# More filler matmuls in the head, and the last tile's large residual add on Pool

## The chip, the cores and the metric

The kernel runs on one core of one Trainium2 chip. A core has five engines with a queue each: PE (TensorE, matmuls), DVE (VectorE), ACT (ScalarE), POOL (GpSimd) and SP, which here only issues DMAs. They run side by side and wait for each other through semaphores. The metric is the device time of one execution in microseconds; the time given is the median over repeated runs. The profile is of one execution.

## The reference

With x of shape [2048, 1024], 32 heads of 32 and bf16 data, the kernel computes

```
xn  = layernorm(x)
q, k, v = split(xn @ wqkv)                       # 32 heads x 32
logits[s, w] = q[s] . k[s - 2w] / sqrt(32)       # w = 0..7, masked where s - 2w < 0
s   = (softmax(logits) over v[s - 2w]) @ wo      # 1024 x 1024
h   = silu(xn @ w1) * (xn @ w3)                  # 1024 -> 3584
g   = silu(h @ w2)                               # 3584 -> 1024
out = x + s * g
```

## The kernel before

The 2048 rows are done in four chunks of 512 (`CH`), each of four tiles of 128 rows (`st`). For a chunk, PE makes q, k and v from the transposed normalized rows `xnT`, then the gate and up products in 14 blocks (`up_block`), then the down product in two halves of 512 output columns (`down_half`), with the attention's output projection (`wo_piece`) in the middle. The attention arithmetic, the layer norm of the next chunk and the closing `x + s * g` are put between PE's groups from a list with costs and due times (`Side`); the program order on each engine is the order in which the code issues the instructions (`manual_schedule`). Weights are streamed by SP through nine buffers. Nothing of this middle part is touched.

*The head* (lines 525 to 583) is written out by hand. There is nothing for PE to compute until the first rows of x are loaded and normalized, so `busy(src, n)` (line 492) issues n filler matmuls, 128 x 512, whose result lands in the PSUM tile `warm_ps` and is never read. Fourteen of them stand at the start. Then comes tile 0: its statistics and normalization on VectorE (`half_stats`, `aggr`, `norm0`, the normalization itself is line 193), eight transposes on PE (`pe_transpose`, line 517), and copies of the transposes from PSUM into `xnT` (`copy_in`, line 521). Six fillers follow the transposes of tile 0. Tile 1 goes the same way, and then the first matmuls of q start on these two tiles (`part`, line 563), with the transposes of tiles 3 and 2 between them. The PSUM pool of `warm_ps`, the transposes and `ps_wo` has two buffers.

*The tail* is `last_half`: for the last chunk, the second half of the down product is made one row tile after another (line 477). For each, ScalarE applies silu out of PSUM (`silu_acc`, line 428), and `finish` does three things: VectorE multiplies with the attention output (line 434), VectorE adds the rows of x (line 435) into a buffer `o_t`, and a DMA on the given queue writes it out (line 436). For the last row tile the output projection is done at the very end, in a piece of 384 columns and one of 128, each followed by its own `finish`; VectorE reads the projection straight from PSUM. Both pieces are written out by the SP queue, the 384-column piece first.

Of the kernel before, what the change touches and what calls it, by code (L numbers as in the profile page):

```python
# [45 lines left out]
def kernel(  # L46
# [11 lines left out]
    nc = tc.nc  # L58
# [4 lines left out]
    CH = 512  # L63
    NCH = S // CH
    NST = CH // P
# [73 lines left out]
    def take_w(item):  # L139
        got, wt = w_tiles.popleft()  # L140
        assert got == item, (got, item)
        return wt
# [6 lines left out]
    x0 = [xp.tile([P, D], BF16, tag="x", name=f"x0_{st}") for st in range(NST)]  # L149
# [39 lines left out]
    def half_stats(x_t, stats, i):  # L189
        nc.vector.bn_stats(out=stats[:, i, :], in_=x_t[:, i * 512:(i + 1) * 512])  # L190
# [214 lines left out]
    def wo_piece(oT, was, st, c0, w):  # L405
        dh, n0 = divmod(c0, CH)
        ps = psum_aux.tile([P, CH], FP32, tag="aux", name="ps_wo")
        for j in range(NJ):
            nc.tensor.matmul(  # L409
                ps[:, 0:w], lhsT=oT[:, j, st * P:(st + 1) * P], rhs=was[dh][:, j, n0:n0 + w],  # L410
                start=(j == 0), stop=(j == NJ - 1),
            )
        return ps
# [12 lines left out]
    def silu_acc(acc, w=512):  # L426
        gt = ep.tile([P, 512], FP32, tag="gt", bufs=5)
        nc.scalar.activation(out=gt[:, 0:w], in_=acc, func=ACTF.Silu)  # L428
        return gt

    def finish(c, st, c0, w, gt, s, xres, queue):
        g0 = (c * NST + st) * P
        o_t = ep.tile([P, 512], BF16, tag="o_t")
        nc.vector.tensor_mul(gt, gt, s)  # L434
        nc.vector.tensor_add(o_t[:, 0:w], gt, xres[:, st, c0:c0 + w])  # L435
        queue.dma_start(out=out_flat[g0:g0 + P, c0:c0 + w], in_=o_t[:, 0:w])  # L436

    def finish_half(c, dh, gts, s_sb, xres, queue):
        def one(st):
            finish(c, st, dh * 512, 512, gts[st][:], s_sb[:, st, dh * 512:(dh + 1) * 512], xres, queue)  # L440
        for st in range(NST):
            side.add(1.38, lambda st=st: one(st))
# [29 lines left out]
    def last_half(c, hts, s_sb, xres, was):  # L472
        w2ts = [take_w(("2", 1, fb)) for fb in range(7)]
        for st in range(NST):
            acc = psum_mm.tile([P, 512], FP32, tag="mm", name=f"acc{c}_1_{st}")
            for f in range(FT):
                nc.tensor.matmul(  # L477
                    acc[:], lhsT=hts[f][:, st * P:(st + 1) * P], rhs=w2ts[f // 4][:, f % 4, :],
                    start=(f == 0), stop=(f == FT - 1),
                )  # L480
            gt = silu_acc(acc[:])
            if st < NST - 1:
                finish(c, st, 512, 512, gt[:], s_sb[:, st, 512:1024], xres, nc.sync)
        for n0, w in ((0, 384), (384, 128)):
            ps = wo_piece(att["oT"], was, NST - 1, CH + n0, w)
            finish(c, NST - 1, CH + n0, w, gt[:, n0:n0 + w], ps[:, 0:w], xres, nc.sync)


    xnT = xnT_pool.tile([P, KT, CH], BF16, tag="xnT")
# [2 lines left out]
    def busy(src, n):  # L492
        for _ in range(n):
            nc.tensor.matmul(wps[:], lhsT=warm[:, 0:P], rhs=src[:, 0:CH], start=True, stop=True)
# [15 lines left out]
    def norm0(st):  # L510
        nc.vector.reciprocal(out=rs0[st][:], in_=rs0[st][:])
        normalize(x0[st], mv0[st][:, 0:1], rs0[st][:])

    def pe_transpose(st):
        tp = psum_aux.tile([P, KT, P], BF16, tag="aux", name=f"tp{st}")
        for kt in range(KT):
            nc.tensor.transpose(tp[:, kt, :], x0[st][:, kt * P:(kt + 1) * P], ident[:])
        return tp

    def copy_in(tp, st, ks, eng):  # L520
        eng(out=xnT[:, ks, st * P:(st + 1) * P], in_=tp[:, ks, :])
# [10 lines left out]
    half_stats(x0[1], st0[1], 0)  # L532
    norm0(0)
    tp0 = pe_transpose(0)
    busy(x0[0], 6)
    copy_in(tp0, 0, HI, A)
    half_stats(x0[1], st0[1], 1)
    aggr(1)
# [2 lines left out]
    half_stats(x0[3], st0[3], 0)  # L541
    norm0(1)
    tp1 = pe_transpose(1)
    half_stats(x0[3], st0[3], 1)
    copy_in(tp1, 1, LO, V)
    copy_in(tp1, 1, HI, A)
# [38 lines left out]
    for j in range(NOPEN, NJ):  # L585
        ps = psum_mm.tile([P, CH], FP32, tag="mm", name="ps_qkv")
# [5 lines left out]
    for c in range(NCH):  # L592
# [15 lines left out]
        xres = res["x"]  # L608
        every = [(dh, st) for dh in range(2) for st in range(NST)]
        if c + 1 < NCH:  # L610
            state = {}

            def mid(fb):
                if fb == WO_AT - 1:
                    state["s"] = wo_proj(every, was)
                    finish_half(c, 0, gts, state["s"], xres, nc.gpsimd)

            gts1 = down_half(c, 1, hts, mid)
            side.flush()
            finish_half(c, 1, gts1, state["s"], xres, nc.gpsimd)  # L620
            xnT = att["x"]
        else:
            s_sb = wo_proj(every[:-1], was)
            finish_half(c, 0, gts, s_sb, xres, nc.gpsimd)
            side.flush()
            last_half(c, hts, s_sb, xres, was)
# [30 lines left out]
```

## Time and profile before

| what | us |
|---|---|
| median of three runs | 819.64 (818.79 to 819.96) |
| the profiled execution | 818.27 |
| its span, first to last instruction | 816.5 |
| PE busy in the span | 809.6 (99%) |
| VectorE busy | 464.8 (57%) |
| ScalarE busy | 191.5 (23%) |
| Pool busy | 92.4 (11%) |
| first real matmul of q starts | 9.72 |
| last product on VectorE of the last tile starts | 813.13 |

In the lines of the profile that follow, a timeline row has the start in us, the duration in us, the engine, the line of the kernel, the operation, output and inputs by the program's names, the shape, and in brackets the idle time of the engine just before it with what ended it. `x6` means six instructions in one row; the duration is then that of the row. PE is the matmuls, PEld the weight loads that go with them, SPq the issuing of DMAs by SP. In a row of grouped instructions the numbers behind the bar are busy us, mean ns of one, and idle time before. Durations of matmuls include the way through the array: what counts for the next matmul is the distance of the starts.

### The profile page before, as it was taken

To read this page: it belongs to the slowest core of one execution; us is meant where nothing else is said; L and a number is where in the kernel's file an instruction comes from. 1 tells how busy PE (TensorE), PEld (TensorE's weight loads), DVE (VectorE), ACT (ScalarE), POOL (GpSimd) and SP (SyncE) were. 2 spreads that over 40 slices of the span, in tenths; PEclk is the share of its full clock that TensorE was granted. 3 is DMA by queue.
4 is the path that set the end of the run, shared out by engine and by line. 5 is a ranking of instruction groups with operands and counts; after the bars stand their busy time and mean duration, and the time that the engine had idled before them with its cause. 6 is when DMAs were issued, how large, how long until landed. Compare 5 with 4: busy or idle time off the path is not lost.

```text
span 816.5 us, 9525 instructions
## 1 busy us (share of the span) xinstructions
PE 809.6 (99%) x3820; PEld 406.2 (50%) x3820; DVE 464.8 (57%) x472; ACT 191.5 (23%) x310; POOL 92.4 (11%) x172
## 2 busy tenths in 40 slices
PE   8999999999999999999999999999999999999997
PEld 6654444444565444444466444444446644444443
DVE  4099574942229765692224968479311694759432
ACT  4331331012332132101133213310223321311120
POOL 0000312001100223000110031400001004130010
PEclk9999999999999999999999999999999999999999
DMA  8476999742366799965245789996424378687500
GB/s 283 136 197 202 212 182 298 242 155 78 104 192 170 221 197 214 296 207 154 78 132 152 190 221 197 210 291 206 142 90 155 104 206 204 165 220 240 177 33 20
DMA packets 190925, 146.39 MB, mean 179 GB/s; under 512 B 19360, under 2 KB 171680, under 8 KB 190880
## 3 DMA queue, kind: packets, MB, share of 16 engines
q1 hardware_dynamic: 185440, 133.71, 59.1%
q0 software_dynamic: 5440, 12.07, 6.4%
q8 instruction: 30, 0.49, 0.3%
q14 instruction: 15, 0.12, 0.1%
HBM read 130.02 MB, written 4.19 MB: 164 GB/s over the span
## 4 chain that ended last, share of the span: by engine, by line
PE 91%; DVE 4%; DMA 2%; issue 1%; ACT 1%; POOL 0%; SPq 0%; DVEq 0%; ACTq 0%
PE gu L245 40%; PE acc L454 20%; PE ps_qkv L245 19%; PE ps_wo L409 7%; PE acc L477 3%; DMA Pr<-pb 2%; PE ps_qkv L563 1%; DVE pv L383 1%; DVE ht L251 1%; DVE stats L190 1%; POOL Pr L372 0%; DMA x<-in_A_x_dram 0%; ACT L249 0%; DVE oT L394 0%; DVE pv L394 0%
## 5 line engine op out<-in xcount | busy, mean ns | idle before, releaser
L245 PE MATMUL gu<-xnT_next,w 128*128 128x512 bf16 x1344 | 290.6, 379 | 0.0
L245 PEld LDWEIGHTS <-w 128*128 128x128 bf16 x1792 | 175.3, 98 | 211.2
L454 PE MATMUL acc<-w,ht 128*128 128x512 bf16 x784 | 170.5, 379 | 0.1
L245 PEld LDWEIGHTS <-wq 128*128 128x128 bf16 x720 | 103.3, 143 | 52.1
L249 ACT ACTIVATE sg<-gu 128x512 bf16<-128x512 f32 x112 | 65.9, 597 | 261.8 <-PE gu L245 242.7
L251 DVE TENSOR_TENSOR ht<-sg,gu 128x512 bf16<-128x512 bf16 x112 | 75.8, 681 | 88.5 <-PE gu L245 70.0
L299 DVE TENSOR_TENSOR prod<-qT,kT 128x4096 bf16<-128x4096 bf16 x32 | 73.1, 2285 | 92.6 <-ACT kT L272 92.6
L245 PE MATMUL ps_qkv<-xnT_next,wq 128*128 128x512 bf16 x576 | 124.8, 379 | 0.0
L454 PEld LDWEIGHTS <-ht 128*128 128x128 bf16 x784 | 76.6, 98 | 92.9 <-issue 0.4
L245 PE MATMUL gu<-xnT,w 128*128 128x512 bf16 x448 | 96.9, 379 | 0.0
L434 DVE TENSOR_TENSOR gt<-gt,s_sb 128x512 f32<-128x512 f32 x31 | 21.4, 690 | 125.2 <-ACT gt L428 67.7
L330 POOL DMA_DIRECT2D L<-E x64 | 37.2, 588 | 273.5 <-DVE E L314 265.6
L383 DVE TENSOR_TENSOR pv<-Pr,vT 128x4096 bf16<-128x4096 bf16 x28 | 63.3, 2283 | 0.0
L310 DVE TENSOR_TENSOR prod<-prod 128x2048 bf16<-128x2048 bf16 x64 | 61.2, 956 | 1.4
L409 PE MATMUL ps_wo<-wo,oT 128*128 128x512 bf16 (+2 forms) x264 | 56.1, 373 | 0.0
L428 ACT ACTIVATE gt<-acc 128x512 f32<-128x512 f32 x32 | 19.1, 597 | 148.8 <-PE acc L454 127.0
L436 POOL DMA_DIRECT2D out_dram<-o_t x28 | 15.4, 549 | 310.5 <-DVE o_t L435 310.5
L372 POOL DMA_DIRECT2D Pr<-pb x64 | 36.8, 582 | 108.7 <-DVE pb L364 99.9
L409 PEld LDWEIGHTS <-oT 128*128 128x128 bf16 x264 | 25.6, 98 | 30.0
L394 DVE TENSOR_TENSOR oT<-oT,pv 128x4096 bf16<-128x4096 bf16 x16 | 36.6, 2287 | 0.2
L421 ACT CAST s_sb<-ps_wo 128x512 bf16<-128x512 f32 x31 | 18.2, 586 | 66.4 <-PE ps_wo L409 66.4
L245 PE MATMUL ps_qkv<-xnT,wq 128*128 128x512 bf16 x144 | 31.2, 379 | 0.0
(64 smaller groups left out, 312.2 us busy)
## 6 DMA issues: line engine op xcount, KB each, us to landing
w<-in_B_w_dram SPq DMA_DIRECT2D x168, 512.0 KB, 5.2
wq<-in_A_wqkv_dram SPq DMA_DIRECT2D x44, 512.0 KB, 3.8
wo<-in_A_wo_dram SPq DMA_DIRECT2D x8, 1024.0 KB, 10.0
L<-E POOLq DMA_DIRECT2D x64, 64.0 KB, 6.1
Pr<-pb POOLq DMA_DIRECT2D x64, 64.0 KB, 5.1
xres<-in_A_x_dram SPq DMA_DIRECT2D x4, 1024.0 KB, 6.2
out_dram<-o_t POOLq DMA_DIRECT2D x28, 128.0 KB, 2.0
x_t<-in_A_x_dram SPq DMA_DIRECT2D x12, 256.0 KB, 6.6
```

The source lines that it names most:

```text
L245: nc.tensor.matmul(ps, lhsT=lhs(kt), rhs=rhs(kt), start=(kt == 0), stop=(kt == KT - 1))
L249: nc.scalar.activation(out=sg[:], in_=g_ps[:], func=ACTF.Silu)
L251: nc.vector.tensor_mul(ht[:], sg[:], u_ps[:])
L299: nc.vector.tensor_mul(prod, qT[:], kT[:, :, o:o + CH])
L310: nc.vector.tensor_add(prod[:, 0:n, :], prod[:, 0:n, :], prod[:, n:2 * n, :])
L330: nc.gpsimd.dma_start(out=L4[sq * NH:(sq + 1) * NH, r, :, :], in_=E_r[r, :, :, sq * P:(sq + 1) * P],)
L372: nc.gpsimd.dma_start(out=Pr_r[r, :, :, sq * P:(sq + 1) * P], in_=pb[sq * NH:(sq + 1) * NH, :, :],)
L383: nc.vector.tensor_mul(dst, Pr[:, w, :].unsqueeze(1).to_broadcast([P, NJ, CH]), vT[:, :, o:o + CH])
L394: nc.vector.tensor_add(a, a, b)
L409: nc.tensor.matmul(ps[:, 0:w], lhsT=oT[:, j, st * P:(st + 1) * P], rhs=was[dh][:, j, n0:n0 + w], start=(j == 0), stop=(j == NJ - 1),)
L454: nc.tensor.matmul(accs[st][:], lhsT=hts[f][:, st * P:(st + 1) * P], rhs=w2t[:, i, :], start=(f == 0), stop=(f == FT - 1),)
L477: nc.tensor.matmul(acc[:], lhsT=hts[f][:, st * P:(st + 1) * P], rhs=w2ts[f // 4][:, f % 4, :], start=(f == 0), stop=(f == FT - 1),)
```

## The change

Two places are edited. In the head, the fillers behind the transposes of tile 0 become ten instead of six, and two fillers are put behind the transposes of tile 1, reading tile 1. In the tail, `finish` gets an argument for the engine of the residual add; for the last row tile, the add of the 384-column piece is done by Pool and that of the 128-column piece still by VectorE. Both products stay on VectorE, both DMAs on the SP queue in the same order.

```diff
-    def finish(c, st, c0, w, gt, s, xres, queue):
+    def finish(c, st, c0, w, gt, s, xres, queue, adder=None):
         g0 = (c * NST + st) * P
         o_t = ep.tile([P, 512], BF16, tag="o_t")
         nc.vector.tensor_mul(gt, gt, s)
-        nc.vector.tensor_add(o_t[:, 0:w], gt, xres[:, st, c0:c0 + w])
+        (adder or nc.vector).tensor_add(o_t[:, 0:w], gt, xres[:, st, c0:c0 + w])
         queue.dma_start(out=out_flat[g0:g0 + P, c0:c0 + w], in_=o_t[:, 0:w])
...
-        for n0, w in ((0, 384), (384, 128)):
+        for n0, w, adder in ((0, 384, nc.gpsimd), (384, 128, nc.vector)):
             ps = wo_piece(att["oT"], was, NST - 1, CH + n0, w)
-            finish(c, NST - 1, CH + n0, w, gt[:, n0:n0 + w], ps[:, 0:w], xres, nc.sync)
+            finish(c, NST - 1, CH + n0, w, gt[:, n0:n0 + w], ps[:, 0:w], xres, nc.sync, adder)
...
     tp0 = pe_transpose(0)
-    busy(x0[0], 6)
+    busy(x0[0], 10)
     copy_in(tp0, 0, HI, A)
...
     tp1 = pe_transpose(1)
+    busy(x0[1], 2)
     half_stats(x0[3], st0[3], 1)
```

## The prediction

> **What bounds the kernel now.** I read the page's busy table first, then the granted clock, then the two ends of the run, since the change touches nothing between them: the timeline and the chain of the first 10 us, and the timeline of the last 5 us.
>
> ```profile
> PE 809.6 (99%) x3820; PEld 406.2 (50%) x3820; DVE 464.8 (57%) x472; ACT 191.5 (23%) x310; POOL 92.4 (11%) x172
> PEclk9999999999999999999999999999999999999999
> ```
>
> PE is busy 99% of the span at the full clock, so from about 10 us to 812 us the time is PE's queue. Only what delays PE's first real matmul, or what lies behind its last one, moves the end. First the head, TensorE's matmuls and then its weight loads:
>
> ```profile
> 5.73 0.62 PE L517 MATMUL tp<-ident,x 128*128 128x128 bf16 x8
> 6.19 1.46 PE L494 MATMUL warm_ps<-x,warm 128*128 128x512 bf16 x6
> 8.59 0.62 PE L517 MATMUL tp<-ident,x 128*128 128x128 bf16 x8 [0.94 <-DVE x L193]
> ...
> 2.91 0.15 PEld L494 LDWEIGHTS <-warm 128*128 128x128 bf16 x1 [0.28 <-issue]
> 3.34 0.15 PEld L494 LDWEIGHTS <-warm 128*128 128x128 bf16 x1 [0.28 <-issue]
> 3.76 1.48 PEld L494 LDWEIGHTS <-warm 128*128 128x128 bf16 x7 [0.28 <-issue]
> ```
>
> The six fillers stand between the first and second transposes, then PE idles 0.94 us until VectorE has normalized the second tile. The weight loads of the start-up fillers come 0.43 us apart up to 3.76 us and 0.21 us apart after it (seven in 1.48 us): the array runs at half rate for its first 2.5 us. The chain through the same stretch:
>
> ```profile
> 7.78 0.17 DVE rs L511
> 7.96 0.03 issue
> 7.98 0.56 DVE x L193
> 8.54 0.05 issue
> 8.59 0.64 PE tp L517 x8
> 9.22 0.02 issue
> 9.24 0.44 DVE xnT L521
> 9.68 0.04 issue
> 9.72 2.78 PE ps_qkv L563 x24
> ```
>
> PE is on it only with the transposes; from 9.72 us on it is PE's own. The 24 matmuls of 256 columns take 2.78 us, that is 0.11 us each, half of the 0.21 us of 512 columns: full rate, in spite of the idle 0.94 us and of the 0.52 us ahead of them. Last the tail, in the timeline:
>
> ```profile
> 812.06 0.55 DVE L434 TENSOR_TENSOR gt<-gt,ps_wo 128x384 f32<-128x384 f32 x1 [5.37 <-PE ps_wo L409]
> 812.65 0.56 DVE L435 TENSOR_TENSOR o_t<-gt,xres 128x384 bf16<-128x384 f32 x1
> 813.13 0.28 DVE L434 TENSOR_TENSOR gt<-gt,ps_wo 128x128 f32<-128x128 f32 x1
> 813.24 0.86 SPq L436 DMA_DIRECT2D out_dram<-o_t  x2
> 813.44 0.29 DVE L435 TENSOR_TENSOR o_t<-gt,xres 128x128 bf16<-128x128 f32 x1
> ```
>
> Four VectorE operations run in a row. SP issues the 384-column piece at 813.24 us and the 128-column piece when VectorE is through (813.73 us): the two issues end at 814.10, each takes 0.33 us by the rows of the output tensor, so the second starts at 813.77. From there to the end of the span (816.5) are 2.73 us: 1.5 us of landing by the issue table, the rest the closing of the program. I take these 2.73 us as fixed.
>
> **The change part by part.** *Four more fillers after the first transposes.* They are 128x512 matmuls at full rate there: starts 0.216 us apart (six start between 6.19 and 7.27 and each is 0.38 long in the rows, which makes the 1.46). The tenth starts at 6.19 + 9 x 0.216 = 8.13 and has left the array at 8.35. The second transposes wait for VectorE until 8.54 and start at 8.59. Cost 0, covered by the idle 0.94 us; 0.24 us of that cover is left. VectorE's normalization and ScalarE's copies of the first transposes wait for no filler, so nothing on the chain before 8.59 moves. If the cover were gone, each filler would cost its 0.216 us.
>
> *Two fillers after the second transposes.* Eight transposes start 0.056 us apart from 8.59, the last has passed at 9.04. The fillers hold the array from 9.04 to 9.47. VectorE's copy of the transposes is released by the last transpose, not by the fillers, so it keeps 9.24; the first real matmul waits for that copy and starts at 9.72. Cost 0, cover 0.25 us. Behind the fillers stand the weight load of the first wq matmul (0.15 us at 8.99 now; it fits between 9.3 and 9.72) and all of PE's queue. The filler bank is now freed only at about 9.63 instead of 7.65; the next user is the third transposes at 12.34, and the next writer of the second x tile is a load at 73.6 us, so neither waits. Twelve instructions more on PE are inside these sums.
>
> *The 384-column add moved from VectorE to Pool.* VectorE loses 0.56 us: its 128-column product starts at about 812.6 instead of 813.13 and its 128-column add ends at about 813.2. Pool has been idle since its last output DMA at 785.25 + 0.54 us, so it starts when VectorE's product is done: 812.61 plus 0.05 for the signal, 812.66. Pool's other waits (x's residual tile, the older users of the output buffer, whose transfer was issued at 800.68) are long satisfied, and nothing is queued behind the add on Pool. But SP's queue keeps its order: the 384-column DMA now waits for Pool, and the 128-column DMA waits behind it although its data are ready. With T for Pool's add, SP issues the first at 812.68 + T and the second 0.37 us later (0.33 for the issue, 0.04 for the wait), at 813.05 + T. Before, it was 813.77. So the end moves by **T - 0.72 us**.
>
> T is not in the trace. Pool's rows, and VectorE's row for the same operation:
>
> ```profile
> L278 POOL COPY kT<-kT 128x128 bf16<-128x128 bf16 x3 | 0.9, 303 | 0.0
> L641 POOL MEMSET const-float32-0.0<- 128x1 f32 x1 | 0.1, 100 | 0.2 <-issue 0.2
> L435 DVE TENSOR_TENSOR o_t<-gt,xres 128x384 bf16<-128x384 f32 x1 | 0.6, 557 | 0.0
> ```
>
> Lower end: VectorE's pace, 0.56 us, a gain of 0.16. Pool's copy gives 0.10 fixed and (303 - 100)/128 = 1.6 ns per column with one input: 0.10 + 384 x 1.6 ns = 0.71 us, no change. Twice the slope for two inputs: 1.32 us, 0.60 us slower. The add reads two inputs, so it is nearest to the last two rows; I take their middle, T = 1.0 us: **+0.28 us**, with -0.16 and +0.60 as ends. Where VectorE's 128-column add meets Pool's on the memory and waits for it, it ends 0.29 us after Pool, still ahead of SP's second issue slot 0.37 us after Pool.
>
> [...]
>
> *Sum.* 0 + 0 + 0.28 us. The profiled execution took 818.27 us (span 816.5 and 1.77 outside it) and becomes 818.55; the median of the three timed runs is 819.64, 1.37 above it. On the median: **819.9 us**. A difference of 0.2% (1.64 us) is about what a measurement of this kernel can tell from no change, and this one is far inside it.
>
> **The rivals.** *Pool is as quick as VectorE* (T = 0.56): 819.64 - 0.16 = 819.5. For it: Pool's memsets and selects take 0.2 to 0.3 us, no more than VectorE's small operations. Against: its copy of 128 bf16 columns takes 303 ns, more than VectorE's add of 128 (292).
>
> *The fillers overrun the gap* (the other side). The place is the second transposes at 8.59. Here the array reached full rate at 3.8 us; in one us at half rate PE loses 0.49 us of work (2.3 fillers done instead of 4.6). PE is ready for the first transposes 0.10 us early (the fourteenth filler leaves at 5.58, VectorE delivers at 5.68), and the ten fillers leave 0.24. So from a full rate that comes 0.34/0.49 = 0.7 us later, at 4.5 us, the added fillers delay the chain, up to all four at half rate, 4 x 0.43 = 1.7 us: 820.2 to 821.6. For it: start-up is part of every execution. Against: the one execution shown has the cover.
>
> [...] This trace has the half rate for 2.5 us; a later release in other runs is not shown by it.
>
> *The idle time costs clock in the timed runs, and the fillers save it.* The timed runs lie 0.5 to 1.7 us above the profiled one. A fall to half rate as long as that of the start (2.5 us) costs 1.27 us; all of it saved gives 819.92 - 1.27 = 818.6, and a longer fall would give 818.0. For it: that spread. Against: the full rate at 9.72 here.
>
> *Pool's first add has a start-up.* The nearest price of a first use is ScalarE's table load, 1.28 us in the rows of this trace: 821.2, and more if Pool's is dearer. Against: Pool's first copies and selects here show 0.3 us and no gap. [...]
>
> **How the numbers follow.** Forecast (T between 0.7 and 1.3, head hidden) 0.52; Pool quick 0.08; overrun 0.15, of which 0.06 is beyond 821.28; clock saved 0.12, of which 0.06 is below 818.0; start-up 0.13, of which 0.12 is beyond 821.28. Slower 0.06 + 0.12 = 0.18, faster 0.06, within 0.2% the other 0.76. The range runs from the clock saved (818.6) to the middle of the slow cases (821.4); what it leaves out is most of the start-up and the tips of the other two.
>
> **What would show it.** In the changed profile: ten fillers from 6.19 and the second transposes still at 8.59 behind VectorE's normalization; two fillers ahead of 9.72 and matmuls from 9.72; in the tail a Pool add of about 1 us from 812.66, and SP's two issues back to back, the second near 814.05. Wrong it is if the transposes wait for fillers, if PE's matmuls after 9.72 run at 0.21 us each, or if Pool's add is several us long or starts late.

## The result, and the profile after

The changed kernel takes 820.87 us (median of 20 runs, 819.71 to 822.75) against 819.68 us before (20 runs, 818.66 to 820.77). The ratio is 1.0016 with a 95% interval of 1.0009 to 1.0022, that is 0.7 to 1.8 us slower: inside 0.2%, but four times the 0.28 us that the sum gave. The profiled execution has a span of 818.5 us against 816.5 and took 820.30 us against 818.27. So 2.0 us have to be found between these two executions.

The head first: TensorE's matmuls of the changed kernel in the timeline, then the chain of the same stretch.

```profile
5.94 0.62 PE L517 MATMUL tp<-ident,x 128*128 128x128 bf16 x8 [0.22 <-DVE x L193]
6.39 2.32 PE L494 MATMUL warm_ps<-x,warm 128*128 128x512 bf16 x10
8.55 0.61 PE L517 MATMUL tp<-ident,x 128*128 128x128 bf16 x8
9.00 0.59 PE L494 MATMUL warm_ps<-x,warm 128*128 128x512 bf16 x2
```

```profile
5.94 0.62 PE tp L517 x8
6.56 2.16 PE warm_ps L494 x10
8.71 0.46 PE tp L517 x8
9.18 0.02 issue
9.20 0.44 DVE xnT L521
```

The fillers fit, but only just: the idle 0.94 us ahead of the second transposes has become nothing, and the chain now runs through the ten fillers. VectorE delivered the first tile at 5.88 us instead of 5.68 in this execution, which moved the fillers 0.2 us later and used up the cover. VectorE delivered the second tile at 8.43 us, 0.10 earlier than before; the fillers then hold its transposes for about 0.07 us, to 8.55. The first real matmul starts at 9.68 us (9.72 before): the head cost less than 0.1 us here.

The tail of the changed kernel in the timeline:

```profile
812.83 0.75 DVE L434 TENSOR_TENSOR gt<-gt,ps_wo 128x384 f32<-128x384 f32 x2 [5.37 <-PE ps_wo L409]
813.47 0.91 POOL L435 TENSOR_TENSOR o_t<-gt,xres 128x384 bf16<-128x384 f32 x1 [27.80 <-DVE gt L434]
813.61 0.91 DVE L435 TENSOR_TENSOR o_t<-gt,xres 128x128 bf16<-128x128 f32 x1
814.40 0.81 SPq L436 DMA_DIRECT2D out_dram<-o_t  x2
```

Pool's add takes 0.91 us. VectorE's add of 128 columns, which waits for nobody in the program, takes 0.91 us too, instead of 0.29. Counted from the start of the 384-column product (812.06 before, 812.83 now), the two output DMAs are all issued 2.38 us later (814.40 + 0.81 - 812.83) instead of 2.04 (813.24 + 0.86 - 812.06): 0.34 us more. From the same point to the end of the span it is 5.7 us instead of 4.4, 1.2 to 1.3 us more. So about 0.9 us are lost behind the last DMA issue, in the stretch that the prediction took as fixed. The closing instructions, by their line, show them. Columns: number, shortest/median/longest in ns, first and last start. Before:

```profile
L652 POOLq EVENT_SEMAPHORE  x4: 17/17/17, 815.8 to 816.4; - x4
L652 POOLq DRAIN  x3: 40/98/3908, 785.2 to 816.2; - x3
L652 SPq DRAIN  x3: 7/7/7, 815.7 to 816.0; - x3
```

And after:

```profile
L653 POOLq EVENT_SEMAPHORE  x4: 17/17/17, 817.8 to 818.4; - x4
L653 POOLq DRAIN  x3: 40/98/4315, 813.4 to 818.3; - x3
L653 SPq DRAIN  x3: 7/7/7, 816.8 to 818.0; - x3
```

Pool's queue ends with a drain, here an instruction that starts beside Pool's last work and ends well behind it, and the engines meet (the rows of semaphores) only after it. In the changed kernel the drain starts at 813.43 and lasts 4.32 us, to 817.74: Pool's add ended at 814.38, so the drain goes on for 3.36 us behind it. SP has the landings and is ready at 816.8; Pool comes at 817.8. Before, the same drain stands at 785.2 and lasts 3.91 us, to 789.1: Pool's last instruction, a DMA issue, ended at 785.79, again 3.35 us earlier. There it lay 26 us ahead of the end and cost nothing. SP comes 0.35 us later against the product, Pool 0.9 us later than SP: together the 1.2 to 1.3 us.

What is left of the 2.0 us is not in either edit. The changed kernel's timeline has one gap on TensorE in the middle of the run:

```profile
552.39 0.68 DVE L251 TENSOR_TENSOR ht<-sg,gu 128x512 bf16<-128x512 bf16 x1
552.98 2.29 DVE L394 TENSOR_TENSOR oT<-oT,pv 128x4096 bf16<-128x4096 bf16 x1
553.12 1.67 PE L454 MATMUL acc<-w,ht 128*128 128x512 bf16 x7 [0.91 <-DVE ht L251]
```

VectorE made that `ht` 0.76 us later than before (552.39 against 551.63), because it had waited 7.7 us instead of 6.9 for the DMA of `Pr` ahead of 537 us. None of the edits touches this stage, so I take it for a difference between two executions; no run was made for it alone. The other traces bear this out: from the first real matmul to the 384-column product it is 802.34 us in the profile of before and 803.15 in that of the change, and between 802.4 and 803.3 us in the other traces, whatever was edited (but for the last kernel of the table below, whose matmuls start at half rate).

### The profile page after: what moved, and what is told of

Its sections match the earlier page's. It is cut to its first block, busy times and chain, and to the rows that moved or that the text cites. A ratio compares the mean times of both kernels' runs of the same rounds, so it can differ in the third digit from the quotient of the medians.

```text
span 818.5 us, 9463 instructions
## 1 busy us (share of the span) xinstructions
PE 806.8 (99%) x3752; PEld 406.8 (50%) x3826; DVE 464.8 (57%) x471; ACT 191.4 (23%) x310; POOL 92.9 (11%) x173
## 4 chain that ended last, share of the span: by engine, by line
PE 90%; DVE 4%; DMA 2%; issue 2%; POOL 0%; ACT 0%; SPq 0%; DVEq 0%; ACTq 0%
PE gu L245 39%; PE acc L454 20%; PE ps_qkv L245 19%; PE ps_wo L409 7%; PE acc L477 3%; DMA Pr<-pb 2%; PE ps_qkv L564 1%; DVE pv L383 1%; DVE ht L251 1%; DVE stats L190 1%; POOL Pr L372 0%; DMA w<-in_B_w_dram 0%; DMA x<-in_A_x_dram 0%; ACT L249 0%; DVE oT L394 0%
```

## The experiments

All were timed against the kernel before on the same chip. "Product to end" is the time from the start of VectorE's 384-column product to the end of the span, in the profiled execution: it leaves out the head and the middle.

| kernel | median us | before us | ratio (95%) | product to end |
|---|---|---|---|---|
| before | | | | 4.4 |
| the change | 820.87 | 819.68 | 1.0016 (1.0009 to 1.0022) | 5.7 |
| fillers alone | 819.56 | 819.24 | 1.0005 (0.9997 to 1.0014) | 4.4 |
| Pool add alone | 820.15 | 819.24 | 1.0013 (1.0004 to 1.0022) | 5.7 |
| idle Pool copy | 820.57 | 819.24 | 1.0016 (1.0007 to 1.0025) | 5.3 |
| Pool add one tile earlier | 818.96 | 819.24 | 0.9997 (0.9988 to 1.0005) | 4.5 |
| sixteen fillers | 820.70 | 819.05 | 1.0021 (1.0013 to 1.0030) | 4.4 |
| Pool adds the 128 columns | 820.78 | 819.05 | 1.0024 (1.0015 to 1.0033) | 6.05 |
| second DMA on ScalarE's queue | 820.53 | 819.05 | 1.0016 (1.0007 to 1.0025) | 5.7 |
| no fillers behind tile 0 | 819.63 | 819.05 | 1.0012 (1.0003 to 1.0021) | 4.4 |
| ten at the start, six | 818.96 | 819.37 | 0.9994 (0.9985 to 1.0004) | 4.4 |
| ten at the start, four | 819.12 | 819.37 | 1.0000 (0.9991 to 1.0009) | 4.4 |
| eight at the start, none | 820.69 | 819.37 | 1.0018 (1.0008 to 1.0029) | 4.4 |

### The two parts, each alone

```diff
-    busy(x0[0], 6)
+    busy(x0[0], 10)
...
     tp1 = pe_transpose(1)
+    busy(x0[1], 2)
```

> The fillers alone (ten behind the first transposes, two behind the second), both adds of the tail on VectorE. Theory (the tail makes the difference, by the drain of Pool at the close): the second transposes start at most 0.1 us after VectorE delivers, the first real matmul at 9.6 to 9.8 us, the median within 0.2 us of before. Rival (the fillers delay PE by a late start of the full rate): 0.8 to 1.2 us slower than before, with the fillers on the chain and the real matmuls starting at 10.5 us or later.

By the times, the fillers alone cost -0.25 to +1.15 us: no difference that can be told, and not enough for the whole. But the profiled execution shows what the rival had described. The chain through its head:

```profile
2.69 4.58 PE warm_ps L494 x11
7.26 0.45 PE tp L517 x8
7.71 2.16 PE warm_ps L494 x10
9.87 0.46 PE tp L517 x8
```

And two of the weight loads, with the first transposes behind them:

```profile
5.89 0.15 PEld L494 LDWEIGHTS <-warm 128*128 128x128 bf16 x1 [0.28 <-issue]
6.32 0.15 PEld L494 LDWEIGHTS <-warm 128*128 128x128 bf16 x1 [0.28 <-issue]
6.75 0.15 PEld L517 LDWEIGHTS <-x 128*128 128x128 bf16 x1 [0.28 <-DVE mv L505]
```

All fourteen start-up fillers ran 0.43 us apart; the first record of the full clock is at 7.0 us instead of 3.9. The first transposes start at 7.10, and the ten fillers hold the second ones until 9.71, although VectorE had delivered at 9.31: 0.4 us lost to the added fillers, in this execution. With six fillers the late clock costs less: in the kernel with the early Pool add, below, the full clock came at 6.8 us, the first transposes stood at 7.00, the second at 9.26, right behind VectorE's 9.21, and the first real matmul at 10.40. So neither expectation had the head right: the real matmuls started at 10.83, as the rival said, but the larger part of that delay is the late clock, which six fillers meet too.

```diff
-        nc.vector.tensor_add(o_t[:, 0:w], gt, xres[:, st, c0:c0 + w])
+        (adder or nc.vector).tensor_add(o_t[:, 0:w], gt, xres[:, st, c0:c0 + w])
...
-        for n0, w in ((0, 384), (384, 128)):
+        for n0, w, adder in ((0, 384, nc.gpsimd), (384, 128, nc.vector)):
```

> The Pool add alone, six fillers as before. Drain theory: Pool's add of 0.91 us, then a drain on Pool's queue of about 3.37 us behind it, and the closing waits for that drain: Pool ends 0.9 + 3.4 = 4.3 us after VectorE's product, against 3.1 us from the product to the closing of before, so 1.2 us slower than before. Rival (the price is the longer add and SP's order alone): second output DMA 0.35 us later and 0.35 us slower in all.

The Pool add alone is 0.3 to 1.8 us slower and has the same 5.7 us from product to end as the whole change. Its tail and its closing lines:

```profile
812.34 0.75 DVE L434 TENSOR_TENSOR gt<-gt,ps_wo 128x384 f32<-128x384 f32 x2 [5.37 <-PE ps_wo L409]
812.98 0.91 POOL L435 TENSOR_TENSOR o_t<-gt,xres 128x384 bf16<-128x384 f32 x1 [27.12 <-DVE gt L434]
```

```profile
L652 POOLq EVENT_SEMAPHORE  x4: 17/17/17, 817.3 to 817.9; - x4
L652 POOLq DRAIN  x3: 40/98/4315, 812.9 to 817.8; - x3
L652 SPq DRAIN  x3: 7/7/7, 816.3 to 817.5; - x3
```

SP is ready at 816.3, Pool at 817.3. The time is in the tail, and the larger part of it is the wait for Pool.

### A Pool instruction that no output waits for

```diff
         for n0, w in ((0, 384), (384, 128)):
             ps = wo_piece(att["oT"], was, NST - 1, CH + n0, w)
             finish(c, NST - 1, CH + n0, w, gt[:, n0:n0 + w], ps[:, 0:w], xres, nc.sync)
+            if n0 == 0:
+                nc.gpsimd.tensor_copy(out=spare[:], in_=gt[:, 0:8])
```

> Before, with a Pool copy of 8 columns of the 384-column product into a spare buffer that nobody reads; it is extra work and no output waits for it. Drain theory: the copy takes 0.1 to 0.2 us from 812.7, the drain lasts to about 816.2 us, Pool then comes 0.4 to 0.5 us after SP, and the run is 0.4 to 0.5 us slower than before although the output DMAs stand where they stood. Rival (only what the output waits for counts): no difference from before.

```profile
813.26 0.55 DVE L435 TENSOR_TENSOR gt<-gt,ps_wo 128x384 f32<-128x384 f32 x1 [5.37 <-PE ps_wo L410]
813.85 0.56 DVE L436 TENSOR_TENSOR o_t<-gt,xres 128x384 bf16<-128x384 f32 x1
813.88 0.58 POOL L489 COPY spare<-gt 128x8 f32<-128x8 f32 x1 [27.12 <-DVE gt L435]
814.43 0.85 SPq L437 DMA_DIRECT2D out_dram<-o_t  x2
```

```profile
L655 POOLq EVENT_SEMAPHORE  x4: 17/17/17, 817.9 to 818.5; - x4
L655 POOLq DRAIN  x3: 40/98/3963, 813.9 to 818.3; - x3
```

The output DMAs stand where they stood (all issued 814.43 + 0.85 - 813.26 = 2.02 us after the product's start, 2.04 before), and yet the end comes 0.9 us later and the run is 0.6 to 2.0 us slower. The drain ends 3.36 us behind the copy, as behind the add. This rules out that the add's length or SP's order is the main price. The sum behind 0.4 to 0.5 us was short because the copy of eight columns took 0.58 us where I had put 0.1 to 0.2: it ends 0.05 us after VectorE's add beside it.

In the trace of the change it was the other way round: VectorE's add of 128 columns, 0.91 instead of 0.29 us, ended beside Pool's add, at 814.52, 0.15 us after Pool's 814.38. In both traces the instruction that started second ended just after the other engine's. What holds it up no trace shows, and no run has that copy with VectorE idle beside it.

### The same add, early enough

```diff
-                finish(c, st, 512, 512, gt[:], s_sb[:, st, 512:1024], xres, nc.sync)
+                finish(c, st, 512, 512, gt[:], s_sb[:, st, 512:1024], xres, nc.sync, nc.gpsimd if st == 2 else None)
```

> Pool adds the residual of the tile before the last (512 columns, at 806 us), VectorE both pieces of the last tile. Drain theory: Pool's add takes about 1.2 us and the drain ends at about 810.7 us, 5 us before the closing: within 0.2 us of before. Rival (a Pool add costs wherever it stands, by a start-up or by holding up VectorE): slower by 0.5 us or more.

```profile
806.81 1.15 POOL L435 TENSOR_TENSOR o_t<-gt,xres 128x512 bf16<-128x512 f32 x1 [20.17 <-DVE gt L434]
```

```profile
L652 POOLq EVENT_SEMAPHORE  x4: 17/17/17, 816.6 to 817.2; - x4
L652 POOLq DRAIN  x3: 40/98/4562, 806.8 to 817.0; - x3
```

Here Pool's add ends at 807.96 and the drain at 806.76 + 4.56 = 811.3, 3.4 us behind it and 5 us before the engines meet (816.6). The time does not differ from before. A Pool add costs nothing that can be told here, where its drain is covered, and no start-up price shows.

### The other piece, and the other queue

```diff
-        for n0, w, adder in ((0, 384, nc.gpsimd), (384, 128, nc.vector)):
+        for n0, w, adder in ((0, 384, nc.vector), (384, 128, nc.gpsimd)):
```

> VectorE adds the 384 columns, Pool the 128 columns of the last piece; six fillers. Drain theory: Pool starts when the 128-column product is done (about 0.8 us later than with the 384 columns), adds for 0.35 to 0.5 us, and its drain of 3.37 us ends about 4.7 us after the 384-column product, so 1.4 to 1.7 us slower than before, although the last DMA is issued only 0.1 to 0.2 us later. Rival (the length of Pool's add and SP's order set the price): 0.1 to 0.3 us slower.

```profile
814.02 1.10 SPq L436 DMA_DIRECT2D out_dram<-o_t  x2
814.33 0.43 POOL L435 TENSOR_TENSOR o_t<-gt,xres 128x128 bf16<-128x128 f32 x1 [28.34 <-DVE gt L434]
```

```profile
L652 POOLq DRAIN  x3: 40/98/3817, 814.3 to 818.6; - x3
```

The add is less than half as long (0.43 us), the last DMA is out 0.2 us later than before by product time, and the run has the largest ratio of the table: 1.2 to 2.7 us slower, 1.6 us in the trace (6.05 against 4.4). Pool ends later, at 814.76, and the drain with it, at 818.1.

```diff
-            finish(c, NST - 1, CH + n0, w, gt[:, n0:n0 + w], ps[:, 0:w], xres, nc.sync, adder)
+            finish(c, NST - 1, CH + n0, w, gt[:, n0:n0 + w], ps[:, 0:w], xres, nc.sync if n0 == 0 else nc.scalar, adder)
```

> The Pool add of the 384 columns, with the 128-column piece written out by the ScalarE queue, so that it does not wait behind the 384-column DMA on SP; six fillers. Drain theory: the outputs are issued 0.4 us earlier than with the Pool add on one queue, and the end does not move against it: still 1.1 to 1.3 us slower than before. Rival (SP's order sets the price): 0.4 us better than with one queue.

```profile
813.27 0.75 DVE L434 TENSOR_TENSOR gt<-gt,ps_wo 128x384 f32<-128x384 f32 x2 [5.37 <-PE ps_wo L409]
814.85 0.33 SPq L436 DMA_DIRECT2D out_dram<-o_t  x1
815.00 0.38 ACTq L436 DMA_DIRECT2D out_dram<-o_t  x1
```

Both outputs are issued by 2.11 us after the product's start instead of 2.38, 0.27 us earlier (0.4 were expected; VectorE's add of 128 columns, again 0.91 us beside Pool's, holds the rest: it ends at 814.96, and ScalarE's queue issues at 815.00). The end does not move: 5.7 us. SP's order is not what sets it.

### The fillers and the clock

```diff
-    busy(x0[0], 6)
+    busy(x0[0], 16)
...
     tp1 = pe_transpose(1)
+    busy(x0[1], 2)
```

> Sixteen fillers behind the first transposes and two behind the second, both adds on VectorE. With a cover of 0.24 us behind ten fillers (before) or none (the changed kernel's trace), six more at 0.216 us delay the second transposes, and with them the first real matmul, by 1.05 to 1.35 us: 1.0 to 1.4 us slower than before. Rival (PE's queue in the head is hidden by something else, such as the loads of wq): less than 0.5 us slower.

```profile
6.35 3.62 PE L494 MATMUL warm_ps<-x,warm 128*128 128x512 bf16 x16
9.80 0.61 PE L517 MATMUL tp<-ident,x 128*128 128x128 bf16 x8
10.93 0.81 PE L564 MATMUL ps_qkv<-xnT,wq 128*128 128x256 bf16 x6
```

The first real matmul moves from 9.72 to 10.93, 1.21 us, and the run is 1.1 to 2.5 us slower. Nothing hides PE's queue in the head once the gap is filled.

```diff
-    busy(x0[0], 6)
```

> Before, without the six fillers behind the first transposes: PE idles about 2.4 us ahead of the second transposes. If idle time there costs clock, the first matmuls of q run at half rate (0.21 us for 256 columns instead of 0.11) and the run is 0.5 to 1.3 us slower. If it does not, no difference from before, and the four added fillers could not have gained anything either.

The profiled execution is untouched: first matmuls at 9.70, 24 of them in 2.81 us. But the runs fall into two groups. Seven of eleven lie between 819.15 and 820.08 us with a mean granted clock of 0.999 or 1.000, four between 821.04 and 821.34 with 0.997 or 0.998. By an estimate from the half rate of these traces, a clock of 0.998 over 818 us is about 3.3 us at half rate, 1.6 us of work. All 33 runs of before beside them lie below 820.5 with 0.999 or more. The profile is of a run of the first group, so no trace shows where in the other four the half rate lies. Nor does 0.998 alone prove it: the mean also counts the closing, where the recorded clock fell to half at 816.25 us in the trace of the change, 3.1 us after the end of the last matmul (0.55 from 816 us to the end), and the kernels with a longer closing have runs at 0.998 that are no slower than their others (four of eleven with two queues). Here the closing is as short as before, 4.4 us.

```diff
-    busy(warm, 14)
+    busy(warm, 8)
...
-    busy(x0[0], 6)
```

> Eight start-up fillers and none behind the first transposes: PE is idle for most of the time from 4.6 to 9.7 us. If busy time in the head is what brings and keeps the full rate, most runs have a mean granted clock of 0.998 or less, the first matmuls of q run at 0.21 us for 256 columns, and the median is 1 to 2 us slower than before. If not, no difference from before.

```profile
5.77 1.04 PE L517 MATMUL tp<-ident,x 128*128 128x128 bf16 x8 [0.94 <-DVE x L193]
8.46 1.04 PE L517 MATMUL tp<-ident,x 128*128 128x128 bf16 x8 [1.65 <-DVE x L193]
10.10 4.12 PE L562 MATMUL ps_qkv<-xnT,wq 128*128 128x256 bf16 x22 [0.61 <-DVE mv L505]
```

The matmuls of q run at half rate, 4.12 us for 22, and the first record of the full clock is at 13.3 us. The run is 0.7 to 2.4 us slower, as expected. The mean clock was expected at 0.998 or less in most runs; six of eight had 0.999 or 1.000. Half rate up to 13.3 us would make the mean about 0.992 over this span of 820 us, and the profiled run has 0.999: the mean counts the time from the first record of the full clock on (3.9 us in the trace of before, whose clock is listed as 1.000), so this late start does not show in it; the pace of the matmuls does.

```diff
-    busy(warm, 14)
+    busy(warm, 10)
```

> Before, with ten start-up fillers instead of fourteen; the six behind the first transposes stay. Reading of the traces so far: in some executions the full rate comes only at 5 to 7 us, the fourteen start-up fillers at 0.43 us each then hold PE up to 7.1 us, and the first transposes start up to 1.4 us late. Ten of them are through by 1.23 + 10 x 0.43 = 5.5 us even at half rate, so the first transposes start at 5.7 to 6.0 us whenever VectorE delivers; 0.2 to 0.6 us faster than before in the median. Rival (fewer fillers lose the full rate, as without the six): a group of runs 2 us slower with a mean granted clock of 0.998, and no gain in the median.

Ten start-up fillers free PE in time: the full clock came at 7.1 us in its profile, and the first transposes started at 5.79, right behind VectorE. But the second ones came at 9.18, because ScalarE had waited until 6.30 us for the third tile's load, and VectorE's second tile hangs on ScalarE's queue: its `rs` waited 0.73 us for ScalarE's, up to 8.38. The median is 0.4 us below before; the interval (-1.2 to +0.3 us) does not tell it from no gain. None of its eleven runs shows 0.998.

```diff
-    busy(warm, 14)
+    busy(warm, 10)
...
-    busy(x0[0], 6)
+    busy(x0[0], 4)
```

> Ten start-up fillers and four behind the first transposes. Reading as for ten and six, and where the full rate comes late four fillers at half rate (1.7 us) end before the second tile is normalized, so 0.2 to 0.6 us faster than before. Rival: the longer idle time ahead of the second transposes costs the full rate in some executions, 2 us each, as seen in 4 of 11 runs without fillers.

No gain that can be told (-0.7 to +0.7 us), and one of eleven runs at 821.22 us with a clock of 0.998. But two of the 25 runs of before beside it, with fourteen and six fillers, show the same: 820.87 and 821.02 us at 0.998. So this does not show that four are too few, and it shows that six do not always keep the clock either.

## Why the prediction was right or wrong

*The range and the sign held*: 820.87 lies in 818.6 to 821.4, within 0.2% of before and above it. That was in part luck. The sum put the change at +0.28 us against 1.19; the range reached up to 821.4 for fillers that overrun and for a start-up of Pool, and what filled it was in the main neither. The missing 0.9 us have, in the main, one cause.

*The term that failed* is the sentence that took the 2.73 us from the last DMA issue to the end of the span as fixed: "1.5 us of landing by the issue table, the rest the closing of the program". The closing is not fixed. It waits for Pool's drain, which ends 3.35 to 3.37 us after Pool's last instruction in twelve of the thirteen traces, be that a DMA issue, an add of 128, 384 or 512 columns or a copy of 8; in the thirteenth (ten at the start, four) it is 3.49 behind a DMA issue. In all thirteen the span ends 0.76 to 0.78 us after the later of two: SP ready with the landings, or Pool's drain. The prediction asked what would be queued behind the add on Pool and answered "nothing"; the drain was queued there. It stood in the profile of before, 3.9 us long at 785.2 us, among the closing instructions, 26 us ahead of the end and so covered by everything. Adding an instruction behind 785 us moved that drain; the idle copy, the early add and the 128-column add show that its place sets the price, not the add. What the drain does in its 3.4 us no trace shows.

*The rest of the tail's sum came out.* T was put at 1.0 us between 0.56 and 1.32; it is 0.91. The second output was predicted 0.28 us later and the issues ended 0.34 us later. That they come so close is partly chance: with the measured T the sum gives 0.19, and Pool's start, the step between SP's two issues and the second issue itself each came out 0.04 to 0.06 us longer than put. Against VectorE's 0.557 us for the same add, Pool's 0.907 us is a factor of 1.63. Three sizes give 0.43, 0.91 and 1.15 us: 1.9 ns per column and 0.19 us fixed.

*VectorE's second add* was allowed to wait for Pool's. It took 0.6 us longer beside it (0.91 against 0.29 us) and ended 0.15 us after it, not 0.29; that the two meet on the memory no trace shows. It was right that this stays hidden behind SP's order: the add ends at 814.52, and SP's second issue starts at 814.83.

*The head* was predicted at nothing with a cover of 0.24 us. In the profiled execution the cover was gone and the cost still under 0.1 us; by the times of the fillers alone it is between -0.25 and +1.15 us. The overrun rival was seen: in twelve of the thirteen traces the full clock came anywhere from 3.9 to 7.1 us, and in the one with ten fillers and 7.0 us they cost 0.4 us. Its price was put too high at the top (1.7 us), since with the late clock VectorE's second tile came later as well (9.31 us with the fillers alone, 8.53 before). The twelve traces spread the moment over 3.2 us; what sets it they do not show.

*The clock-saving rival* fell in the form given: the fillers alone are no faster, and with the six of before a run that seems to lose clock is rare (2 of 91 whose clock is listed, both about 1.5 us above their median), so four more had next to nothing to save. Without the six it was 4 of 11 runs, some 2 us each: they are not idle decoration.

*Pool's start-up* does not show here: the first add of the early-tile kernel took 1.15 us and no time was lost. The chance put nearly all of it beyond 821.28, on a price above the 1.28 us of ScalarE's table load; no run shows such a price.

Together: 1.2 to 1.3 us of the tail, of which the prediction had 0.3, and a head that cost under 0.1 us in one trace and 0.4 in another, fit the 1.2 us (0.7 to 1.8) of the medians. The head's share in the median stays open.

## What to carry to other kernels

Before giving an engine work near the end of a program, look at what closes its queue: in all thirteen traces the span ended 0.76 to 0.78 us after the later of SP's landings and Pool's drain, and in the trace of before the drain, over at 789.1 us, was hidden. From the drain's 3.35 to 3.37 us I estimate that a Pool instruction which ends less than 3.4 us before SP is ready with the last landings costs time, even one whose result nobody reads: the copy of 8 columns ended at 814.46, 2.4 us before SP's 816.9, and its run was 0.6 to 2.0 us slower. Fillers on TensorE are a balance. With too few the full clock came late (13.3 us with eight and none) or some runs were 2 us slower (4 of 11 without the six); too many stood in the way of the work they wait for (sixteen moved the first real matmul by 1.21 us). And because the full clock came anywhere from 3.9 to 7.1 us in the other twelve traces, one trace's gap is not the gap of all.

## What the runs showed of the hardware that was not expected

- Pool's closing drain ended 3.35 to 3.37 us after the last Pool instruction in twelve of thirteen traces (3.49 in one), whatever that was.
- A Pool copy of 8 columns took 0.58 us beside a VectorE add of 384 columns (0.56 us), and a VectorE add of 128 columns 0.91 instead of 0.29 us beside a Pool add.
- TensorE's full clock came between 3.9 and 7.1 us after the start with fourteen or ten start-up fillers, and at 13.3 us with eight and none behind.
